# Two fused layers on one NeuronCore: head sums by ScalarE's accumulator, block products on copied partial sums, four batches' tails together, batch 0 in units, and a new order of all steps

## The chip, the cores and the metric

The kernel runs on one core of a Trainium2 chip. The core has five engines with a queue of instructions each: TensorE (PE) multiplies and transposes into the eight PSUM banks; VectorE (DVE) and ScalarE (ACT) do element work and read and write PSUM and SBUF; GpSimd (POOL) works on SBUF; SyncE (SP) issues most DMA transfers. ScalarE's and GpSimd's queues issue some transfers too. Every queue is worked off in order; semaphores hold an instruction until what it needs is done.

The metric is the device time of one execution in microseconds (us), lower is better. The kernel before takes 295.43 us, the median of 3 runs (295.1 to 296.01).

## The reference

Batch 8, 8 heads of 64, sequence 576, width C = 512; activations are float32, `w_val`, `conv_w` and `w_out` arrive as float64.

```python
kv = einsum('bhsd,bhse->bhde', k, v)
out = einsum('bhsd,bhde->bhse', q, kv)
rms = sqrt(mean(out * out, axis=-1, keepdims=True) + 1e-06)
x = (out / rms * g_norm), heads side by side          # (B, S, 512)
gate_pre[:, t] = sum over k of conv_w[k] * x[:, t - 4 + k]   # 5 taps, causal
gate = 1 / (1 + exp(-gate_pre))
val = x @ w_val
return gate * val @ w_out
```

## The kernel before

All work is written as small steps, Python functions such as `fast_product(i, p, n)`. A text, `PLAN` (lines 19 to 226), lists 1242 of them, with the buffers they take behind an `@`. The loop at the end walks this list and issues each step's instructions. So the list sets both the order in each engine's queue and the order of any two accesses to one buffer. `rooms` (line 275) holds the buffers by tag: eight PSUM banks (`bank`), rooms for gates, normalised rows (`x`), squares (`sq`) and so on.

A batch goes through these steps. Tokens come in chunks c = 0 to 3 of 128 and a tail, c = 4, of 64.

- `load_half` and `load_q` (or `load_q_rows` for batches 0 and 1) fetch k, v and q. `kv_product` (line 468) sums k^T v per head, 36 small products per half of the heads; `kv_copy` takes the result out. For batch 0 `kv_half` lays it out block by block in `kv_bd`.
- q is turned by TensorE (`turn_q_rows`, then `sort_q` copies) for batches 0 and 1 and by VectorE (`turn_q`) later on.
- `raw_pair` and `raw_tail` (batch 0: `raw_half`) multiply q by kv into two banks. `square` (line 583) squares the heads on ScalarE into a `sq` room whose 65th column per head holds the epsilon, `sums` (line 604) adds up each head on VectorE, `powers` (line 613) raises to -1/2 on GpSimd, and `normalise` (line 620) multiplies: on ScalarE one instruction per head, with the head's root as its scale; for batch 0 on VectorE.
- The normalised rows are turned into `xT` (channels on partitions): by `turn_x` and `keep_x` for batches 0 and 1 and all tails, by `turn_blocks` on VectorE and `move_blocks` otherwise. `move_blocks` issues four transfers, on GpSimd's and SyncE's queues in turn.
- `gate_start`, four `gate_tap` and `gate_end` make a gate per 128 channels.
- val: for batches 0 and 1 `val_product` (line 695), plain products. For batches 2 to 7 a scheme with seven block products in place of eight: `x_sums` and `val_sums` make sums of blocks, `val_fast` n = 0 to 6 (line 734) multiplies into three banks a, b, c, and `val_keep` (line 751) takes partial results out between products. Product 0 fills a; its copy goes to SBUF; products 2, 4 and 6 add onto a and each state is read again; c is used by products 1 and 5, b by product 3. Reads 3, 4 and 5 are VectorE adds onto the SBUF copy, the others are ScalarE copies.
- `gated` multiplies gate and val.
- Output, for pairs i of batches: `token_sums` and `weight_sums` make block sums, `fast_product` n = 0 to 6 (line 819) multiplies in the same scheme, for four groups p of 256 tokens per pair. Half bank a has a bank of its own; b and c are two halves of another (`both`, line 834). `fast_keep` (line 842) reads: ScalarE copies for n = 0, 1, 2, 6; VectorE adds for 4 (256 wide) and 5 (512 wide, b and c at once). The two 64-token tails of a pair go through `out_product` (line 772, eight products of 512 columns) and `keep_out`. `store` writes rows out in four transfers, mostly on SyncE's queue.

The float64 weights come as pairs of 32-bit words (`stage_weight`) and are made float32 by `narrow_weight` in eight steps: 0, 4, 5, 6, 7 on VectorE, 1, 2, 3 on ScalarE. `start_warm` issues products of the identity as a filler for TensorE.

Of the kernel before, what the change touches and what calls it, by code (L numbers as in the profile page):

```python
# [9 lines left out]
FP32 = mybir.dt.float32  # L10
# [5 lines left out]
P = 128  # L16
# [3 lines left out]
load_q_rows 0 1; load_q_rows 0 0; load_half v 0 0 @ 0; load_half k 0 0 @ 0; load_half v 0 1 @ 0;  # L20
load_half k 0 1 @ 0; start_warm 5 256 @ 0; warm_up; stage_weight wval 0; stage_weight wval 1;
stage_weight cw 0 @ 0; turn_q_rows 0 4 @ 1; turn_q_rows 0 3 @ 2; sort_q 0 4 @ 0; turn_q_rows 0 0 @ 3;
turn_q_rows 0 2 @ 4; sort_q 0 3; turn_q_rows 0 1 @ 5; start_warm 3 256 @ 6; load_q_rows 1 0; load_q_rows 1 1;
sort_q 0 0; stage_weight wval 2; kv_product 0 0 @ 7 0; narrow_weight cw 0 0 @ 0; load_half k 1 1; sort_q 0 2;
load_half v 1 1; kv_half 0 0; sort_q 0 1; raw_half 0 3 0 @ 1; narrow_weight cw 0 1; narrow_weight cw 0 2;
kv_product 0 1; stage_weight wval 3; narrow_weight cw 0 3; load_half k 1 0; narrow_weight cw 0 4;
narrow_weight cw 0 5 @ 0; raw_half 0 0 0 @ 2; stage_weight wout 1 @ 1; narrow_weight cw 0 6 @ 1; kv_half 0 1;
narrow_weight cw 0 7; narrow_weight wval 0 0 @ 1; raw_half 0 3 1; narrow_weight wval 0 5 @ 2;
narrow_weight wval 0 1; raw_half 0 0 1; narrow_weight wval 0 6 @ 3; turn_cw @ 6; square 0 3 @ 0;
raw_half 0 2 0 @ 3; keep_cw; square 0 0 @ 1; sums 0 3 @ 0 0; raw_half 0 2 1; narrow_weight wval 0 2;  # L30
raw_half 0 4 1 @ 4; sums 0 0; powers 0 3; load_half v 1 0; square 0 2 @ 2; raw_half 0 4 0;
narrow_weight wval 1 0 @ 0; raw_half 0 1 0 @ 5; square 0 4 @ 0; sums 0 2; narrow_weight wval 0 3;
raw_half 0 1 1; sums 0 4; load_half v 2 1 @ 0; start_warm 1 256 @ 0; narrow_weight wval 1 1;
narrow_weight wval 0 4; powers 0 2; square 0 1 @ 1; narrow_weight wval 1 5 @ 0; narrow_weight wval 1 2;
narrow_weight wval 0 7; stage_weight wout 0 @ 2; turn_q_rows 1 3 @ 7; normalise 0 3 @ 0;
narrow_weight wval 1 3; turn_q_rows 1 2 @ 6; sums 0 1; sort_q 1 3 @ 1; turn_q_rows 1 1 @ 0;
load_half v 2 0 @ 0; narrow_weight wval 2 0 @ 1; turn_x 0 3 @ 1; narrow_weight wval 1 6 @ 1; powers 0 1;
normalise 0 4 @ 1; narrow_weight wval 2 1; turn_q_rows 1 0 @ 7; load_q 2 2; normalise 0 2 @ 2; turn_x 0 4 @ 4;
keep_x 0 3; narrow_weight wval 1 4; turn_x 0 2 @ 3; keep_x 0 4; narrow_weight wval 2 2;
narrow_weight wval 2 5 @ 2; kv_product 1 1 @ 1 4; narrow_weight wval 1 7; keep_x 0 2;  # L40
narrow_weight wval 2 6 @ 3; sort_q 1 1; val_product 0 1 1 @ 3; narrow_weight wval 3 0 @ 0;
narrow_weight wval 3 5 @ 0; halo 0; normalise 0 1 @ 0; narrow_weight wval 3 1; normalise 0 0 @ 1;
narrow_weight wval 2 3; narrow_weight wval 3 6 @ 1; turn_x 0 1 @ 0; narrow_weight wval 3 2; turn_x 0 0 @ 5;
narrow_weight wval 2 4; load_half k 2 1 @ 0; val_product 0 0 1 @ 2; keep_x 0 1; narrow_weight wout 1 5 @ 2;
keep_x 0 0; narrow_weight wval 2 7; narrow_weight wval 3 3; narrow_weight wout 1 0 @ 1;
narrow_weight wout 1 6 @ 0; gate_start 0 0 @ 0; kv_product 1 0; narrow_weight wval 3 4; gate_start 0 3 @ 1;
gate_tap 0 0 3; sort_q 1 2; turn_q_rows 1 4 @ 0; narrow_weight wval 3 7; val_product 0 0 0 @ 5; load_q 2 0;
gate_tap 0 0 2; keep_val 0 0 1; gate_tap 0 3 3; gate_start 0 1 @ 2; sort_q 1 4; val_sums 2;
val_product 0 3 0 @ 6; gate_tap 0 1 3; kv_copy 1 1; kv_copy 1 0; load_q 2 1; sort_q 1 0; gate_tap 0 0 1;
raw_tail 1 @ 0 2; gate_tap 0 3 2; raw_pair 1 3 @ 1 4; square 1 4 @ 2; narrow_weight wout 0 5 @ 3;  # L50
keep_val 0 0 0; gate_tap 0 0 0; val_product 0 2 1 @ 7; gate_start 0 2 @ 3; gate_tap 0 3 1; square 1 3 @ 0;
square 1 2 @ 1; sums 1 4 @ 1 1; gate_tap 0 2 3; narrow_weight wout 1 1; powers 1 4; load_half k 2 0 @ 0;
val_product 0 1 0 @ 5; sums 1 3; keep_val 0 1 1; stage_weight wout 3 @ 0; gate_end 0 0; gate_tap 0 1 2;
powers 1 3; narrow_weight wout 1 2; sums 1 2; narrow_weight wout 1 3; val_product 0 2 0 @ 3; gated 0 0;
keep_val 0 3 0; keep_val 0 2 1; gate_tap 0 2 2; normalise 1 4 @ 2; powers 1 2; narrow_weight wout 1 4;
normalise 1 3 @ 0; raw_pair 1 1 @ 7 6; turn_q 2 0 @ 0; stage_weight wout 2 @ 1; turn_q 2 2; turn_x 1 4 @ 0;
load_q 2 3; val_product 0 3 1 @ 2; gate_tap 0 3 0; keep_x 1 4; normalise 1 2 @ 1; gate_tap 0 2 1;
narrow_weight wout 0 6 @ 2; turn_x 1 3 @ 0; keep_val 0 3 1; gate_tap 0 1 1; load_q 3 1; turn_x 1 2 @ 1;
# [172 lines left out]
def kernel(  # L231
# [104 lines left out]
    def head(hp, r):  # L336

        return r * (H // 2) + hp
# [579 lines left out]
```

## Time and profile before

| what | value |
|---|---|
| median of 3 runs | 295.43 us (295.1 to 296.01) |
| the profiled execution: span from first to last instruction | 294.9 us |
| mean granted TensorE clock | 0.993 |
| `fast_product` rows (L838), 448 | about 381 ns as a row, overlapping |
| `val_fast` rows (L747), 336 | about 407 ns as a row |
| `out_product` rows (L785), 64 | 598 ns as a row |
| `normalise` on ScalarE (L636), 252 | 56.1 us busy |
| `square` on ScalarE (L600), 70 | 21.6 us busy |
| `sums` on VectorE (L607), 40 | 24.7 us busy |
| `powers` on GpSimd (L617), 38 | 73.1 us busy |
| `gate_tap` on VectorE (L686), 128 | 100.4 us busy |
| ScalarE busy from 27 to 60, 60 to 105, 105 to 165, 165 to 225 us | 31.69, 36.99, 42.25, 41.05 us |
| VectorE busy in the same stretches | 32.49, 44.60, 59.65, 58.72 us |
| DMA read and written | 39.21 and 9.44 MB |

A profile is one execution recorded on the chip. A row such as "L838 PE MATMUL bank<-wsum,w 128x256 x4" stands for four instructions of line 838 that write a bank from the tiles wsum and w. A float32 product gives two rows. Rows of one engine can overlap: an instruction starts before the one ahead has left the pipeline, so the distance from start to start is what an engine needs for it, and a row is longer. "<-" behind a wait names what ended it. Slices are fortieths of the span, in tenths of busy time.

### The profile page before, as it was taken

How to read it: one execution, taken by the hardware profiler on the slowest of the kernel's cores; microseconds unless marked ns; L12 is line 12 of the kernel's file. 1: busy time of each engine (PE TensorE's matmuls, PEld its weight loads, DVE VectorE, ACT ScalarE, POOL GpSimd, SP SyncE). 2: the span in 40 equal slices, each digit the busy share in tenths (PEclk: the TensorE clock that was granted, in tenths of full speed). 3: DMA queues.
4: the chain of work that ended last, by engine and by line, in shares of the span. 5: the costliest groups of instructions: out<-in, count | busy, mean ns of one | idle time of the engine just before them, and what ended most of it. 6: DMA issues, size and time to landing. Idle time of an engine off the chain costs nothing.

```text
span 294.9 us, 8675 instructions
## 1 busy us (share of the span) xinstructions
PE 287.0 (97%) x3279; PEld 226.9 (77%) x3279; DVE 268.7 (91%) x483; ACT 198.7 (67%) x621; POOL 120.7 (41%) x131
## 2 busy tenths in 40 slices
PE   7999999999999999999999999999999999999994
PEld 3776878788887768878887767888887588788583
DVE  1699999999999999999999999999998999999812
ACT  2899999999786667867477576659588433723330
POOL 3067054854491477421881649021592072000020
PEclk9997999999999999999999999999999999999999
DMA  7999998886686766946789789534553170221344
GB/s 268 379 392 410 284 276 230 239 258 176 197 189 198 234 150 182 341 144 174 182 237 279 167 218 308 165 112 109 141 128 80 44 170 2 57 53 36 98 105 120
DMA packets 32009, 55.51 MB, mean 188 GB/s; under 512 B 6166, under 2 KB 14358, under 8 KB 31968
## 3 DMA queue, kind: packets, MB, share of 16 engines
q1 hardware_dynamic: 29328, 49.50, 57.2%
q0 software_dynamic: 1760, 3.43, 5.2%
q10 hardware_dynamic: 880, 2.03, 1.8%
q8 instruction: 26, 0.43, 0.6%
q14 instruction: 15, 0.12, 0.1%
HBM read 39.21 MB, written 9.44 MB: 165 GB/s over the span
## 4 chain that ended last, share of the span: by engine, by line
PE 94%; DMA 2%; ACT 1%; DVE 1%; issue 0%
PE bank L838 33%; PE bank L747 28%; PE bank L698 11%; PE bank L476 7%; PE bank L551 6%; PE bank L785 5%; PE bank L648 2%; DMA qs<-in_q_dram 2%; PE bank L563 2%; PE bank L515 1%; PE bank L464 0%; ACT wexp L409 0%; DVE x L626 0%; ACT sq L596 0%; DVE ss L607 0%; ACT wexp L407 0%
## 5 line engine op out<-in xcount | busy, mean ns | idle before, releaser
L617 POOL TENSOR_TENSOR rt<-ss,mhalf 128x8 f32<-128x8 f32 (+3 forms) x38 | 73.1, 1937 | 82.0 <-DVE ss L607 81.8
L686 DVE SCALAR_TENSOR_TENSOR gate<-xT,cwT,gate 128x576 f32<-128x576 f32 x128 | 100.4, 807 | 0.2
L636 ACT ACTIVATE x<-bank,rt 128x64 f32<-128x64 f32 x252 | 56.1, 375 | 3.5 <-POOL rt L617 3.2
L838 PE MATMUL bank<-wsum,w 128*128 128x256 f32 x192 | 47.3, 381 | 0.0
L669 POOL DMA_DIRECT2D xT<-y x48 | 26.6, 559 | 41.6 <-DVE gv L754 13.5
L838 PEld LDWEIGHTS bank<-wsum,w 128*128 128x128 f32 x192 | 36.0, 190 | 6.1 <-issue 0.8
L747 PE MATMUL bank<-xs,vsum 128*128 128x288 f32 x144 | 37.1, 407 | 0.0
L747 PEld LDWEIGHTS bank<-xs,vsum 128*128 128x128 f32 x144 | 27.3, 190 | 7.3
L698 PE MATMUL bank<-xT,wval 128*128 128x288 f32 x128 | 32.8, 411 | 0.0
L838 PE MATMUL bank<-wout,gv 128*128 128x256 f32 x128 | 32.3, 382 | 0.0
L698 PEld LDWEIGHTS bank<-xT,wval 128*128 128x128 f32 x128 | 24.0, 192 | 6.3
L693 ACT ACTIVATE gate<-gate 128x576 f32<-128x576 f32 x32 | 23.0, 727 | 7.9 <-DVE gate L686 7.8
L838 PEld LDWEIGHTS bank<-wout,gv 128*128 128x128 f32 x128 | 24.0, 190 | 3.5
L680 ACT ACTIVATE gate<-xT,cwT 128x576 f32<-128x576 f32 x32 | 25.2, 804 | 0.9 <-DVE gv L711 0.9
L747 PE MATMUL bank<-xT,wval 128*128 128x288 f32 x96 | 25.7, 406 | 0.0
L600 ACT ACTIVATE sq<-bank 128x256 f32<-128x256 f32 (+1 forms) x70 | 21.6, 400 | 6.0 <-PE bank L551 5.8
L711 DVE TENSOR_TENSOR gv<-gv,gate 128x576 f32<-128x576 f32 x32 | 23.5, 745 | 2.0 <-ACT gate L693 1.5
L607 DVE TENSOR_REDUCE ss<-sq 128x8 f32<-128x520 f32 (+1 forms) x40 | 24.7, 624 | 0.5 <-ACT sq L600 0.4
L848 DVE TENSOR_TENSOR ot<-bank,ot 128x256 f32<-128x256 f32 (+1 forms) x32 | 17.2, 546 | 8.4 <-PE bank L838 4.1
L747 PEld LDWEIGHTS bank<-xT,wval 128*128 128x128 f32 x96 | 18.2, 190 | 4.5
L854 ACT COPY ot<-bank 128x256 f32<-128x256 f32 x16 | 6.0, 376 | 22.6 <-PE bank L838 22.6
L551 PEld LDWEIGHTS bank<-kv,qT 64*64 64x64 f32 x1008 | 16.3, 135 | 4.8 <-issue 2.1
(91 smaller groups left out, 469.4 us busy)
## 6 DMA issues: line engine op xcount, KB each, us to landing
qs<-in_q_dram SPq DMA_DIRECT2D x96, 140.0 KB, 4.0
out_dram<-ot SPq DMA_DIRECT2D x136, 64.0 KB, 1.7
k<-in_k_dram SPq DMA_DIRECT2D x14, 576.0 KB, 4.9
v<-in_v_dram SPq DMA_DIRECT2D x12, 576.0 KB, 5.3
xT<-y POOLq DMA_DIRECT2D x48, 64.0 KB, 2.7
xT<-y SPq DMA_DIRECT2D x48, 64.0 KB, 2.7
y<-in_moe_w_val_dram SPq DMA_DIRECT2D x4, 512.0 KB, 11.9
w<-in_moe_w_out_dram SPq DMA_DIRECT2D x4, 512.0 KB, 7.1
```

Of the source, the lines that this page charges most:

```text
L551: nc.tensor.matmul(st["raw", b, c][r][cols, to * D:(to + 1) * D], st["qT", b][rows, hp, first:first + D], kvs[b % 2][rows, hp, :], start=T ...
L607: nc.vector.reduce_sum(out=st["ss", b][:, FIRST[c]:FIRST[c] + n], in_=st["sq", b, c][:, 0:n], axis=AX.X)
L617: nc.gpsimd.tensor_tensor(out=st["rt", b][:, which], in0=st["ss", b][:, which], in1=mhalf[:, which], op=ALU.pow)
L636: nc.scalar.activation(out=x[:, to * D:(to + 1) * D], in_=raw[:, h * D:(h + 1) * D], func=AF.Copy, scale=root[:, to:to + 1])
L669: (nc.sync if i % 2 else nc.gpsimd).dma_start(out=xTs[b % 2][i * TB:(i + 1) * TB, :, first:first + P], in_=y[a * TB:(a + 1) * TB, i])
L680: nc.scalar.activation(out=gate[:], in_=xTs[b % 2][:, jt, HALO:SX], func=AF.Copy, scale=cwT[:, K - 1, jt:jt + 1])
L686: nc.vector.scalar_tensor_tensor(out=gate[:], in0=xTs[b % 2][:, jt, tap * TB:tap * TB + S], scalar=cwT[:, tap, jt:jt + 1], in1=gate[:], op ...
L693: nc.scalar.activation(out=gate[:], in_=gate[:], func=AF.Sigmoid)
L698: nc.tensor.matmul(val[:], wval[:, kc, jt * P:(jt + 1) * P], xTs[b % 2][:, kc, HALO + n * SV:HALO + (n + 1) * SV], start=(kc == 0), stop=( ...
L711: nc.vector.tensor_tensor(out=both, in0=both, in1=st["gate", b, jt][:], op=ALU.mult)
L747: nc.tensor.matmul(st[bank, "val", b, mj][:], weights_[:, k], tokens()[:, k], start=(n in (0, 1, 3) and k == 0), stop=(k == NK // 2 - 1), ...
L838: nc.tensor.matmul(st[bank, i, p], tokens()[:, k], weights_[:, k], start=(n < 2 and k == 0), stop=(k == NK // 2 - 1), skip_group_check=True)
```

## The change

The list of steps is new (1288 steps), and these parts of the code:

- **Head sums.** For batches 1 to 7 `square` is one ScalarE instruction per head, which squares into a throw-away tile and gives the sum over the head by its accumulator. `sums` stays for batch 0 alone. `powers` gets a GpSimd add of the epsilon.
- **Copied partial sums.** In all groups (`SEEDED_VAL`, `SEEDED_OUT`), the copy of product 0 goes into bank b, and product 3 adds onto it there; read 3 is then a plain copy (for val in place of an add), and read 5 of the output an add of 256 columns. In the output a and c become the halves of one bank, and b has another bank.
- **Tails.** `keep_tail` copies each batch's 64 tail tokens into a tile; four batches give two chunks of 128, which go through the seven products as groups 4 0 and 5 0. `out_product` of tails and `keep_out` leave the list.
- **Batch 0 in units** of two chunks and half the heads: `raw_unit`, `square_unit`, `sums_unit`, `powers_unit`, `normalise_unit`, `turn_unit`, `keep_unit`; batch 0's `val_product` is split into halves that need one half of the heads each. For that, val's blocks are formed of channel blocks 0, 2 and 1, 3 (`EARLY`, `LATE`) in place of 0, 1 and 2, 3.
- **Weights.** `narrow_weight` loses step 3; step 2 is done on VectorE.
- **Engines by step.** Copies, `normalise`, `gate_start` and step 1 of `narrow_weight` take an argument that puts them on VectorE. `move_blocks` becomes two steps, one per queue.
- **Loads at the start.** `stage_weight wval 0` and `load_half v 0 0` now come ahead of q.

```diff
+    ACT_SUMS = (1, 2, 3, 4, 5, 6, 7)
+    SEEDED_OUT = {(0, 1), (1, 2), (4, 0), (2, 1), (3, 1), (0, 2), (2, 2), (1, 0), (3, 2), (1, 3), (0, 0), (1, 1), (0, 3), (2, 0), (3, 0), (2, 3), (3, 3), (5, 0)}
+    SEEDED_VAL = {(4, 0), (7, 1), (2, 1), (3, 1), (6, 1), (7, 0), (2, 0), (5, 1), (3, 0), (5, 0), (6, 0), (4, 1)}
...
+    EARLY, LATE = slice(0, NK, 2), slice(1, NK, 2)
...
+    def copy(e, out, in_):
+
+        if e:
+            nc.vector.tensor_copy(out=out, in_=in_)
+        else:
+            nc.scalar.copy(out=out, in_=in_)
...
         elif n == 2:
-            nc.scalar.activation(out=e, in_=e, func=AF.Relu, bias=biases[0:rows, 1:2], scale=-1.0)
-        elif n == 3:
-            nc.scalar.activation(
-                out=e, in_=e, func=AF.Identity, bias=biases[0:rows, 2:3], scale=-float(1 << 23))
+            nc.vector.tensor_scalar(
+                out=e, in0=e, scalar1=MOST, scalar2=float(1 << 23), op0=ALU.min, op1=ALU.mult)
...
     def square(b, c):
...
                     nc.scalar.activation(
-                        out=sq[:, to, 0:D], in_=raw[:, h * D:(h + 1) * D], func=AF.Square,
-                        accum_out=st["ss", b][:, FIRST[c] + to:FIRST[c] + to + 1])
+                        out=junk[:], in_=raw[:, h * D:(h + 1) * D], func=AF.Square,
+                        accum_out=st["ss", b][:, first + to:first + to + 1])
...
+    def root(b, which):
+        ss, rt = st["ss", b][:, which], st["rt", b][:, which]
+        if b in ACT_SUMS:
+            nc.gpsimd.tensor_scalar_add(ss, ss, D * EPS)
+        nc.gpsimd.tensor_tensor(out=rt, in0=ss, in1=mhalf[:, which], op=ALU.pow)
...
+    def raw_unit(g, i):
+
+        raw = st["unit", g, i] = ps([P, 2, C // 2], f"unit{g}_{i}")
+        for j, c in enumerate(UNIT[g]):
+            for m in range(2):
+                nc.tensor.matmul(
+                    raw[:, j, m * P:(m + 1) * P], st["qT", 0][:, 2 * i + m, c * P:(c + 1) * P],
+                    kv_bd[:, 2 * i + m, :], start=True, stop=True)
...
-    def move_blocks(b, a):
+    def move_blocks(b, a, e):
...
-        for i in range(HB):
-            (nc.sync if i % 2 else nc.gpsimd).dma_start(
+        for i in range(1 - e, HB, 2):
+            (nc.gpsimd if e else nc.sync).dma_start(
...
     def val_keep(b, mj, n, on=0):
+        seeded = (b, mj) in SEEDED_VAL
+        if seeded and n == 0:
+            st["b", "val", b, mj] = ps([P, SV], f"seed{b}_{mj}")
...
         if n == 0:
-            nc.scalar.copy(out=to(0, 0), in_=a)
+            copy(on, out=b_ if seeded else to(0, 0), in_=a)
...
+        elif n == 3 and seeded:
+            copy(on, out=to(0, 0), in_=b_)
...
+    def keep_tail(b, on=0):
+
+        if ("tail", b // 2) not in st:
+            st["tail", b // 2] = new("sq", [P, NK, P], FP32, f"tail{b // 2}")
+        first = b % GVS * S + SF
+        copy(
+            on, out=st["tail", b // 2][:, :, b % 2 * T:(b % 2 + 1) * T], in_=gv[:, :, first:first + T])
...
     def fast_product(i, p, n):
...
+        if (i, p) in SEEDED_OUT:
+            if n == 0:
+                both = ps([P, 2, C // 2], f"ac{i}_{p}")
+                st["a", i, p], st["c", i, p] = both[:, 0], both[:, 1]
+            for k in range(NK // 2):
+                nc.tensor.matmul(
+                    st[bank, i, p], tokens()[:, k], weights_[:, k],
+                    start=(n == 0 and k == 0), stop=(k == NK // 2 - 1), skip_group_check=True)
+            return
...
     def fast_keep(i, p, n, on=0):
+        seeded = (i, p) in SEEDED_OUT
+        if seeded and n == 0:
+            st["b", i, p] = ps([P, C // 2], f"b{i}_{p}")[:]
...
         if n == 0:
-            nc.scalar.copy(out=first[:, LOW], in_=a)
+            copy(on, out=b if seeded else first[:, LOW], in_=a)
+        elif n == 3:
+            copy(on, out=first[:, LOW], in_=b)
...
+        elif n == 5 and seeded:
+            add(first[:, HIGH], c)
```

The new list begins, and goes on where the groups of output products meet, like this:

```
stage_weight wval 0; narrow_weight wval 0 0 @ 0; narrow_weight wval 0 5 @ 0; load_half v 0 0 @ 0;
start_warm 1 244 @ 0; narrow_weight wval 0 1 1; narrow_weight wval 0 2; start_warm 1 246 @ 1; start_warm 1 248 @ 2;
...
narrow_weight cw 0 0 @ 1; start_warm 3 256 @ 5; start_warm 5 256 @ 6; load_q_rows 0 0; load_q_rows 0 1;
turn_q_rows 0 3 @ 7; load_half k 0 0 @ 0; narrow_weight cw 0 5 @ 2; stage_weight wval 2; load_half v 0 1 @ 0; warm_up;
...
gate_tap 1 2 3; fast_keep 0 0 1 @ 3; fast_product 0 0 2; fast_keep 0 0 2; gate_tap 1 0 3; move_blocks 2 0 0;
fast_product 0 1 2; move_blocks 2 1 0; turn_q 4 0 @ 0; fast_keep 0 1 2 @ 1; square 3 2; fast_product 0 1 3;
...
fast_keep 3 0 1 @ 2; fast_product 3 1 1; fast_keep 3 1 1 @ 0; fast_product 3 1 2; fast_keep 3 1 2 @ 3;
fast_keep 3 0 2 1 @ 1; token_sums 5 0 3 @ 2; fast_product 3 1 5; token_sums 5 0 2; fast_keep 3 1 5;
```

More of the change, by code (lines that the diff above doesn't have):

```diff
@@ L25 @@
[L25 to L41, printed above, removed]
@@ L52 @@
[L52 to L56, printed above, removed]
@@ L102 @@
-gate_start 2 0 @ 2; token_sums 0 1 0 @ 0; move_blocks 3 2; gate_start 2 2 @ 1; turn_q 4 3; normalise 3 4 @ 2;
-move_blocks 3 1; turn_q 4 1; gate_tap 2 3 3; raw_pair 4 3 @ 2 7; token_sums 0 1 1; move_blocks 3 0;
-gate_tap 2 2 3; raw_pair 4 1 @ 6 5; square 4 3 @ 2; gate_tap 2 2 2; keep_out 0 8 @ 0; fast_product 0 3 0 @ 0;
-square 4 1 @ 1; store 0 8; move_blocks 3 3; sums 4 3 @ 0 0; fast_product 0 3 1 @ 3; sums 4 1;
-fast_keep 0 3 0 @ 1; square 4 0 @ 0; gate_tap 2 3 2; powers 4 1; fast_product 0 3 3; token_sums 0 1 2 @ 2;
```

629 lines of the change are left out of this document (340 added, 289 removed).

## The prediction

> **What bounds the kernel now.** I read the page first: busy times, the slices, then the chain that ended last.
>
> ```profile
> PE 287.0 (97%) x3279; PEld 226.9 (77%) x3279; DVE 268.7 (91%) x483; ACT 198.7 (67%) x621; POOL 120.7 (41%) x131
> ...
> PE   7999999999999999999999999999999999999994
> ...
> DVE  1699999999999999999999999999998999999812
> ACT  2899999999786667867477576659588433723330
> ...
> PE 94%; DMA 2%; ACT 1%; DVE 1%; issue 0%
> ```
>
> TensorE is the bound: 94% of the chain, and every slice but the first and last is full. VectorE is as full from slice 3 to 29, yet all waits of TensorE add up to 3.5 us in the view of waits. So only three things can move the end: TensorE's own work, the time until it runs without gaps, and new waits put into its queue.
>
> Next the chain in order of time, for start and prices.
>
> ```profile
> 0.75 5.27 DMA qs<-in_q_dram
> ...
> 10.20 1.28 PE bank L476 x72
> 11.47 0.19 ACT kvbd L486
> 11.66 0.01 issue
> 11.67 0.22 ACT kvbd L486
> 11.89 0.04 issue
> 11.93 0.94 PE bank L563 x4
> ...
> 27.04 2.47 PE bank L698 x8
> ```
>
> ```profile
> 113.16 2.59 PE bank L838 x12
> ...
> 168.66 3.58 PE bank L785 x16
> ```
>
> Rows L838 are four to a `fast_product`: 2.59/12 x 4 = 0.86 us. One `out_product` is 3.58. TensorE is continuous from 27.0, the first `val_product`. Before it stand 34 transposes (0.11 each), three `kv_product` (1.21), 40 rows of L563 (0.108), ten of L648 (0.11) and 0.17 for `turn_cw`: 12.9 us of work at 27.0, a lag of 14.1. At the other end the last product stops at 290.5, and 4.3 us of copy, issue and store follow.
>
> The third view is the timeline of the last microseconds, for the banks.
>
> ```profile
> 285.82 1.24 PE L838 MATMUL bank<-wsum,w 128*128 128x256 f32 x5
> ...
> 286.90 1.03 PE L838 MATMUL bank<-wout,gv 128*128 128x256 f32 x4
> ...
> 288.01 0.37 ACT L852 COPY ot<-bank 128x256 f32<-128x256 f32 x1 [1.40 <-PE bank L838]
> ```
>
> These are product 1 of group 3 3 (the last four of five rows, done at 287.06), product 3, and the copy of what product 1 made. ScalarE idles 1.40 us and copies only at 288.01, 0.08 after product 3 ends at 287.93. Product 3 writes the other half of that bank, no byte that the copy reads. Product 4 (another bank) is not waited for. Groups 3 1, 3 2 and 2 3 show the same (copy 0.03 to 0.04 after product 3). So an access to one half of a bank is held until what the order lists before it on the other half is done.
>
> **The change, part by part.**
>
> *Tails.* Four `out_product` go: 4 x 3.58 = 14.3. Two groups of seven `fast_product` come: 14 x 0.86 = 12.1. TensorE -2.2. Beside it eight copies `keep_tail` (0.38 each on ScalarE, by L854), eight sums (0.41) and four adds (0.41) on VectorE, hidden below. Store transfers stay 16; four move from POOL's queue to SP's.
>
> *Head sums.* VectorE loses 28 reduces of 0.68 and seven of 0.41: 21.8 us. ScalarE loses 70 squares (21.6 us) and gets 252 of 64 elements, with a sum read out each. The trace has no accumulator. Nearest rows:
>
> ```profile
> 85.20 1.75 ACT L636 ACTIVATE x<-bank,rt 128x64 f32<-128x64 f32 x8 [0.75 <-POOL rt L617]
> ...
> 91.25 1.21 ACT L600 ACTIVATE sq<-bank 128x256 f32<-128x256 f32 x4 [0.47 <-PE bank L551]
> ...
> 103.56 0.48 ACT L600 ACTIVATE sq<-bank 128x128 f32<-128x128 f32 x2
> ```
>
> Start to start, a 64-wide instruction with a column operand takes (1.75 - 0.35)/7 = 0.20, a square 0.27 at 256 and 0.18 at 128, so some 0.13 at 64. Low end 0.13 (reading out is free), high end 0.40 (it costs a second such instruction). I take 0.20, the row of the same shape: 50 us (33 to 101). [...]
>
> ScalarE also loses two of three steps of `narrow_weight` (12.8), three more (2.2), `keep_out` (2.4) and 28 normalises (6.2), and gets 20 + 9 copies (11.3), `keep_tail` (3.0) and four sorts (1.5). 198.7 - 45.2 + 66.2 = 220 us, 75% of the span (203 to 270): nothing on TensorE while it stays below it. Uncovered, it is a rival. `powers` gains 35 adds on POOL (0.2 to 0.3 by the fill and select of the identity), 9 us on an engine 41% busy. From raw product to root a chunk then takes 8 x 0.20 + 0.15 + 0.25 = 2.0 us where two squares and a reduce took 1.35; its two banks are held 0.65 longer. Other products cover that, which stand between each `raw_pair` and the next user of its banks; without them it would be 28 x 0.65 = 18 us.
>
> *VectorE.* Beside the sums it loses 12 adds of 0.44 and half of 16 of 0.68 (9.5 together) and gets about 16 (one `narrow_weight` step, tail sums, copies and normalises moved to it): 253 us. Nothing, since TensorE does not wait for it now.
>
> *Copied partial sums.* Product 3 now adds onto a copy of product 0's result, so it waits for a copy. In the order at least one other product (0.86) lies between product and copy's reader in each such pair; a copy with handing over is below that, so 0. But halves a and c now share one bank, and six of seven products and five reads of a group go through it. I went through the order of steps and counted where a product follows directly on one of its own group with a read of that bank listed between (`fast_product 3 1 1; fast_keep 3 1 1; fast_product 3 1 2; fast_keep 3 1 2; ... fast_product 3 1 5`; `fast_product 2 0 5; fast_keep 2 0 5; fast_product 2 0 4`): 15 places, seven of them in the last 26 us of products. The order of before has none. By the bank rows TensorE has to stand until the read is done, all later products behind it. Price: the gap 11.47 to 11.93 is 0.46 for two copies of 0.41, 0.05 for handing over; a 0.37 copy gives 0.42, the low end. The product's drain (1.03 as a row, 0.86 in sequence) adds up to 0.17, and 0.07 goes from product to ACT: high end 0.66. I take 0.55, as weights can load in the drain: 15 x 0.55 = **+8.3** (6.3 to 9.9). [...]
>
> *Batch 0 in units, new order.* On SP `wval` 0 (0.52 MB) now goes ahead of q, on ACT's queue v 0 0 (0.59), so q (1.18) is complete at 2.3 MB in place of 1.2. The slices moved 268 and 379 GB/s, 1.98 MB by 7.4 us: q lands at about 8.2, not 6.0. Thirteen filler products cover that. k 0 0 and part of v 0 1 follow: 10.6. Then a `kv_product` 1.2, copies 0.9, `raw_unit` 0.9, on ScalarE a sort, a narrowing and the square 1.8, the sum 0.7: the first root starts near 16. POOL then has four roots of 2.0 and one of 1.2: last root 25.2, normalise, turn and keep 2.1 more, so TensorE is continuous from 27.3. By then it has done 36 transposes, two `kv_product`, 40 rows of L563, 18 of L648, `turn_cw` and three half `val_product` (0.97): 15.8, a lag of 11.5. That is -2.6; with the roots ahead of it by the 1 us that the two queues' sharing may save, -3.6. I take **-3.0** (-5 if the roots start at 14; +2.2 if q's delay passes through). `move_blocks` issues the same 96 transfers, POOL's half and SP's half apart; waiting there would hold roots, but POOL has 160 us free.
>
> **Sum**: 294.9 (span of the profiled execution) - 2.2 - 3.0 + 8.3 = 298.0. The median of the runs is 295.4, 0.5 above that execution: **298.5 us**, own range 294 to 302.
>
> **Rivals.**
> 1. *The waits cost nothing* (faster): they fall where TensorE stands anyhow, or halves are not held. 298.5 - 8.3 = 290.2 (287 to 294). For it: VectorE gets 15 us of room, and copies list right behind their products. Against it: four groups show the hold, and a continuous TensorE has no gaps to hide 15 waits. Chance 0.30.
> 2. *ScalarE becomes the bound.* From 27 to 225 the table by stretches gives it 152 us of 198; most head squares fall there: less 21.6, 9 (narrowing) and 6, plus 50 and 12, makes 177. At 0.28 per head it is full; at 0.33 it needs 210, 12 more than there is, of which the bank waits share about a third: 306. Against it: that needs a read-out as long as the square. Chance 0.13.
> 3. *The start is later, not earlier*: q's 2.2 us go through to the end: 298.5 + 3.0 + 2.2 = 303.7. For it: VectorE narrows weights between units' sums in one queue. Against: the roots' chain has the later end. Chance 0.10.
> The forecast keeps 0.47.
>
> **How the numbers follow.** A difference of 0.3% (0.9 us) is about what a measurement of this kernel tells from none. Faster: rival 1's 0.28 and 0.05 from the forecast's low end, 0.33. Same: 0.02 and 0.08, 0.10. Slower: 0.57. The range 288.5 to 305 leaves out the best part of rival 1 (0.09) and most of rival 2 (0.10).
>
> **What would show it.** Bank waits: in the waits, TensorE (or its weight loads) on ScalarE's and VectorE's reads at L838's successor, some 15 of 0.5 us, half of them in the last 30 us; if they sum to under 3 us, this step is wrong. Start: first `val_product` near 23, no gap after 27. Head sums: the square's rows 0.20 apart; ScalarE busy near 220, VectorE near 253. Tails: no 512-wide output product left. The prediction fails if TensorE's waits are as few as before, or if ScalarE is full from 30 to 200.

## The result, and the profile after

The changed kernel takes 351.08 us (median of 4 runs, 350.65 to 353.48) where the kernel before takes 295.72 (295.1 to 296.44): a ratio of 1.189, 95% interval 1.185 to 1.193. The forecast was 298.5. The profiled execution has a span of 349.2 us. Some executions of a kernel came out over 1.5% slower than its fastest; the medians of the runs below leave these out, the ranges hold all.

The page of the changed kernel, its busy times, slices and chain:

```profile
PE 300.9 (86%) x3283; PEld 235.9 (68%) x3283; DVE 257.7 (74%) x475; ACT 247.3 (71%) x1043; POOL 121.6 (35%) x164
...
PE   8799799889589948978789887987999999999794
...
DVE  3799499679659937887798797977789998653221
ACT  1889799999689995979988999698945553231210
...
PEclk9999899999899996999999999998999999999999
...
ACT 35%; PE 34%; DVE 16%; DMA 6%; issue 5%; POOL 1%; SPq 0%; DVEq 0%; ACTq 0%
```

TensorE's slices are no longer all 9: they have holes up to slice 26. The chain, 94% TensorE before, is now a third ScalarE. Most of ScalarE's slices up to 26 are at 8 or 9, and that is where TensorE's holes are. The granted clock, flat before but for one slice, has more dips. VectorE's work is what the prediction said (257.7 us for 253), ScalarE's is not (247.3 for 220).

The view of waits of the changed kernel (engine and line, what it waited for, us in total, times, longest):

```profile
PE bank L913 <- ACT bank L345: 10.0, 4, 6.1
PE bank L913 <- ACT ot L345: 10.0, 8, 3.9
...
DVE qT L509 <- DMA qs<-in_q_dram: 9.5, 4, 4.7
...
PE bank L913 <- DVE ot L937: 4.8, 5, 1.2
...
PE bank L485 <- issue: 2.8, 3, 1.2
```

Before, TensorE's waits summed to 3.5 us. Now its block products (L913) wait 20 us for ScalarE's copies (L345) and 4.8 for VectorE's adds (L937). Two rows have no counterpart before: VectorE waits for loads of q, and TensorE stands with nothing waited for ("issue").

The table by stretches, changed kernel (stretch, its length, then busy us and instructions of PE, PEld, DVE, ACT and POOL, the granted clock, DMA share and GB/s):

```profile
27.00:60.00 33.00, 28.68 (x535) 22.73 (x536) 27.71 (x56) 30.01 (x133) 15.22 (x19) 0.95 0.79 247
60.00:105.00 45.00, 36.03 (x531) 27.82 (x522) 31.44 (x56) 39.87 (x207) 24.19 (x31) 0.96 0.86 230
105.00:165.00 60.00, 50.60 (x735) 39.36 (x735) 46.22 (x79) 51.91 (x237) 27.33 (x41) 0.94 0.69 192
165.00:225.00 60.00, 52.28 (x671) 41.41 (x673) 50.33 (x87) 53.40 (x234) 29.89 (x41) 1.00 0.53 149
```

TensorE loses 30 of these 198 us, where before it lost none.

To see where the time goes, I worked out a lag for several kernels: the time less TensorE's useful work done by then. Each recorded row counts with its line's median distance from start to start, and the rows that come in quick pairs with the mean within a step: 17 ns for the 64x64 products, 224 for `out_product`. Warm-up products are left out.

| us from the start | before | changed | five outputs (e1) | places parted (e3) | before, own outputs (e4b) |
|---|---|---|---|---|---|
| 27 | 13.8 | 13.9 | 13.9 | 13.9 | 12.4 |
| 45 | 14.8 | 19.2 | 19.4 | 19.4 | 14.8 |
| 60 | 14.8 | 21.0 | 21.1 | 21.8 | 16.9 |
| 105 | 15.2 | 34.0 | 29.7 | 30.1 | 25.6 |
| 165 | 15.3 | 48.0 | 38.2 | 36.9 | 28.8 |
| 225 | 15.8 | 57.6 | 42.7 | 41.8 | 31.5 |
| 285 | 16.1 | 65.3 | 45.1 | 42.9 | 34.4 |

The kernel before hardly lags further once it is under way. The changed kernel is level with it at 27 us, behind by 4 at 45, and loses most between 60 and 225.

### The profile page after: what moved, and what is told of

It is laid out like the page before. It is cut to its first block, busy times and chain, and to the rows that moved or that the text cites. A ratio compares the mean times of both kernels' runs of the same rounds, so it can differ in the third digit from the quotient of the medians.

```text
span 349.2 us, 9163 instructions
## 1 busy us (share of the span) xinstructions
PE 300.9 (86%) x3283; PEld 235.9 (68%) x3283; DVE 257.7 (74%) x475; ACT 247.3 (71%) x1043; POOL 121.6 (35%) x164
## 4 chain that ended last, share of the span: by engine, by line
ACT 35%; PE 34%; DVE 16%; DMA 6%; issue 5%; POOL 1%; SPq 0%; DVEq 0%; ACTq 0%
PE bank L913 22%; ACT junk L606 17%; PE bank L809 8%; DVE gate L747 7%; ACT x L657 6%; DMA qs<-in_q_dram 3%; DMA k<-in_k_dram 3%; ACT qT L345 2%; ACT gate L742 2%; ACT gv L345 2%; DVE gv L772 2%; PE bank L562 2%; ACT ot L345 2%; DVE ot L937 1%; PE bank L671 1%
## 5 line engine op out<-in xcount | busy, mean ns | idle before, releaser
L913 PE MATMUL bank<-wsum,w 128*128 128x256 f32 x216 | 58.2, 400 | 21.1 <-ACT bank L345 10.0
L629 POOL TENSOR_TENSOR rt<-ss,mhalf 128x8 f32<-128x8 f32 (+1 forms) x40 | 68.7, 1722 | 19.0 <-DVE ss L682 16.1
L606 ACT ACTIVATE junk<-bank 128x64 f32<-128x64 f32 x252 | 57.5, 228 | 9.8 <-PE bank L562 2.5
L913 PEld LDWEIGHTS bank<-wsum,w 128*128 128x128 f32 x216 | 41.8, 200 | 32.4 <-ACT bank L345 12.4
L345 ACT COPY ot<-bank 128x256 f32<-128x256 f32 x65 | 25.3, 400 | 39.5 <-PE bank L913 35.5
L606 ACT ACTIVATION_READ_ACCUMULATOR junk<-bank 128x1 f32 x252 | 50.5, 200 | 0.0
L628 POOL TENSOR_SCALAR ss<-ss 128x8 f32<-128x8 f32 (+1 forms) x35 | 12.1, 346 | 83.0 <-ACT junk L606 82.0
L345 ACT COPY gv<-bank 128x288 f32<-128x288 f32 x61 | 26.1, 440 | 17.9 <-PE bank L809 17.9
L937 DVE TENSOR_TENSOR ot<-bank,ot 128x256 f32<-128x256 f32 x36 | 15.0, 419 | 28.6 <-PE bank L913 17.0
L913 PE MATMUL bank<-wout,gv 128*128 128x256 f32 x128 | 35.2, 403 | 0.4 <-DVE gv L772 0.4
L913 PEld LDWEIGHTS bank<-wout,gv 128*128 128x128 f32 x128 | 25.4, 201 | 5.8 <-DVE gv L772 1.2
L760 PEld LDWEIGHTS bank<-xT,wval 128*128 128x128 f32 x128 | 24.1, 195 | 6.6 <-ACT kv L345 0.2
L719 DVE STREAM_TRANSPOSE y<-x 128x512 f32<-128x512 f32 x24 | 16.8, 705 | 9.8 <-ACT x L657 9.8
```

Source lines behind the costliest of these rows:

```text
L345: nc.scalar.copy(out=out, in_=in_)
L606: nc.scalar.activation(out=junk[:], in_=raw[:, h * D:(h + 1) * D], func=AF.Square, accum_out=st["ss", b][:, first + to:first + to + 1])
L629: nc.gpsimd.tensor_tensor(out=rt, in0=ss, in1=mhalf[:, which], op=ALU.pow)
L760: nc.tensor.matmul(st["val", b, jt, n][:], wval[:, kc, jt * P:(jt + 1) * P], xTs[b % 2][:, kc, HALO + n * SV:HALO + (n + 1) * SV], start=( ...
L913: nc.tensor.matmul(st[bank, i, p], tokens()[:, k], weights_[:, k], start=(n == 0 and k == 0), stop=(k == NK // 2 - 1), skip_group_check=True)
L937: add = lambda out, one: nc.vector.tensor_tensor(out=out, in0=one, in1=out, op=ALU.add)
```

## The experiments

T1: ScalarE's head sums are dearer than taken and hold up what stands behind them. T2: the waits at the bank that a and c share. T3: the new order, its start and its queues. T4, formed later: TensorE runs out of instructions. T5, later: loads of q late in SyncE's queue hold up VectorE and with it TensorE. Times are medians; the kernel before took 295.4 to 295.5 beside each.

### Head sums: one output or several

What the trace showed first is the distance of two heads. ScalarE's timeline in the changed kernel (start, us, operation):

```profile
40.26 0.23 ACT L606 ACTIVATE junk<-bank 128x64 f32<-128x64 f32 x1
40.38 0.19 ACT L606 ACTIVATION_READ_ACCUMULATOR junk<-bank 128x1 f32 x1
40.61 0.22 ACT L606 ACTIVATE junk<-bank 128x64 f32<-128x64 f32 x1
```

A head is two instructions: the square, and 0.12 us later a read-out of 0.19. The next square starts 0.35 after the last, only when the read-out has ended. All heads write one tile, `junk`, and in the program each next square waits on the semaphore that the one before it raises; in the trace it starts 0.04 behind the end of the read-out (40.57 to 40.61). Four kernels test whether this wait is the price.

e1, five outputs in turn:

```diff
-    junk = const.tile([P, D], FP32, name="junk")
+    junk = const.tile([P, 5, D], FP32, name="junk")
...
-                        out=junk[:], in_=raw[:, h * D:(h + 1) * D], func=AF.Square,
+                        out=junk[:, to % 5], in_=raw[:, h * D:(h + 1) * D], func=AF.Square,
```

> The changed kernel, but the 252 head squares write five 64-wide outputs in turn instead of one. T1 (a head costs 0.35 us because each square waits for the read-out of the one before, whose output it overwrites, and ScalarE so loaded holds up the copies): the step from head to head falls from 0.347 to about 0.21 us (0.12 to the read-out, 0.093 behind it), ScalarE's heads from 87 to about 54 us, the time from 351 to about 320 us (308 to 330). T1b (the read-out itself lasts that long whoever follows): the step stays at 0.33 to 0.35 and the time at 348 to 354. T2 (the waits on the shared bank alone made the loss) and T3 (the new order and start made it): the step falls but the time stays above 343.

Measured: 329.9 us (329.3 to 331.3), 21.2 below the changed kernel. ScalarE's timeline of e1 at that time:

```profile
40.12 0.22 ACT L606 ACTIVATE junk<-bank 128x64 f32<-128x64 f32 x1
40.23 0.21 ACT L606 ACTIVATION_READ_ACCUMULATOR junk<-bank 128x1 f32 x1
40.32 0.23 ACT L606 ACTIVATE junk<-bank 128x64 f32<-128x64 f32 x1
```

The next square now starts 0.09 behind the start of the read-out: a step of 0.20 us in place of 0.35. ScalarE is busy for 225.5 us, near the 220 forecast. So T1 holds for the step, T1b falls. But 329.9 is 10 us above the 320 that T1 expected, at the upper end of its range.

e4a and e4b put the head sums alone into the kernel before: `ACT_SUMS = (1, 2, 3, 4, 5, 6, 7)`, no `sums` for these batches, order as before. e4a writes all heads of a chunk to one place, e4b each to its own columns:

```diff
-                        out=sq[:, to, 0:D], in_=raw[:, h * D:(h + 1) * D], func=AF.Square,
+                        out=sq[:, 0, 0:D], in_=raw[:, h * D:(h + 1) * D], func=AF.Square,
```

> The kernel before with one part of the change: head sums of batches 1 to 7 by ScalarE's accumulator, all heads of a chunk written to one 64-wide output, VectorE's reductions of these batches gone, order and all else as before. T1: the step from head to head is 0.35 us, ScalarE is full between 60 and 225 us, the time rises from 295.7 to about 330 us (315 to 345). T2 and T3: the time stays within 291 to 303.

> As the run with one output a chunk, but every head of a chunk writes columns of its own. T1: the step is about 0.21 us, heads take 54 us in place of the 16 of wide squares, and the time is 295 to 312 us, well under that of the run with one output. T1b: the step stays at 0.33 to 0.35 and both runs agree within 2 us. T2 and T3: 291 to 303.

Measured: e4a 353.8 us (+58.4, ratio 1.199, interval 1.195 to 1.203), e4b 315.6 (+20.2, 1.070, 1.067 to 1.072). The head sums alone, written as in the changed kernel, cost the old order more than the whole change costs, and 38 us of it is the shared output. T1 is shown. e4a's own timeline shows both steps beside each other:

```profile
41.69 0.22 ACT L385 ACTIVATE sq<-bank 128x64 f32<-128x64 f32 x1
41.81 0.19 ACT L385 ACTIVATION_READ_ACCUMULATOR sq<-bank 128x1 f32 x1
41.90 0.22 ACT L385 ACTIVATE sq<-bank 128x64 f32<-128x64 f32 x1
```

Within a chunk the squares are 0.35 apart. The one at 41.90 begins a new chunk, which writes another tile, and it starts 0.21 behind the square before it.

e4b also shows something T1 had too small: at 0.20 a head, the price I had taken, the sums still cost 20 us. e4b by stretches:

```profile
27.00:60.00 33.00, 29.81 (x466) 23.14 (x465) 27.02 (x48) 32.75 (x147) 12.32 (x15) 1.00 0.86 256
60.00:105.00 45.00, 38.46 (x546) 30.12 (x546) 33.65 (x57) 42.03 (x234) 23.24 (x28) 1.00 0.63 175
```

ScalarE, with 230 of 314 us busy in the whole, is full here (32.75 of 33, 42.03 of 45), and TensorE loses 10 us. e4c and e4d ask whether that is the reason: heads on ScalarE only in batches 3 to 7, or only in 1 and 2.

> As the run of the kernel before with own outputs for the heads (315.6 us, 20.2 above the kernel before), but head sums on ScalarE in batches 3 to 7 alone (180 of the 252 heads); batches 1 and 2 keep wide squares and VectorE's sums. T1 (it costs where ScalarE is full: 32.8 of 33 us from 27 to 60 and 42.0 of 45 from 60 to 105, where batches 1 and 2 lie): 300 to 305. Rival (each head costs the same wherever it lies): 295.4 + 20.2 x 180 / 252 = 309.8.

> The counterpart: head sums on ScalarE in batches 1 and 2 alone (72 heads). T1: 305 to 311. Rival (each head costs the same): 295.4 + 20.2 x 72 / 252 = 301.2.

Measured: 307.0 us for 180 late heads (+11.6, 0.064 a head) and 305.3 for 72 early ones (+9.9, 0.138 a head). An early head costs twice a late one, so the full stretch matters: e4d's TensorE is busy without a break from 105 to 285 us, so all its loss lies before. But late heads are not free either, and e4c lies between the two expectations. Its ScalarE is busy for 77 to 86% of the stretches from 60 to 225 us, and yet TensorE stops there 1.1 us for a norm of ScalarE and 1.3, 1.4 and 1.9 us for its copies. These four stops are about half of the 11.6 us; where the rest arises is not shown.

e2 takes ScalarE's load away from the changed kernel itself; it forms one sum per bank and leaves out the sums per head:

```diff
-                for h in range(n // 2):
-                    to = r * n // 2 + h
-                    nc.scalar.activation(
-                        out=junk[:], in_=raw[:, h * D:(h + 1) * D], func=AF.Square,
...
+                to = r * n // 2
+                nc.scalar.activation(
+                    out=junk[:, 0:n // 2 * D], in_=raw[:, 0:n // 2 * D], func=AF.Square,
```

> The changed kernel, but one square with one accumulator for each bank of heads (70 of them, 256 or 128 wide) instead of one for each head; the other sums of a bank are left at 1, so the norms are left out in part, and every other instruction stays. T1: ScalarE gives up about 87 - 70 x 0.45 = 55 us, the time falls to 300 to 315 us. T2 or T3: the time stays above 340, since the order and the 15 places at the shared bank are untouched.

Measured: 325.6 us (325.6 to 332.0; the median rests on one execution), 4 below e1, though ScalarE is busy for 204 us in place of 225. Both expectations miss: T1 alone would have given 300 to 315. Once a head takes 0.20, ScalarE's load is worth a few us at most in the new order. Something else holds it some 30 us above the kernel before.

### Bank places parted

e3 is e1 with another product put between at 15 of the 18 places where a product follows one of its own group with a read of the bank that a and c share in between, as here (the prediction counted 15; in three more the product ahead is one that fills b):

```diff
-fast_product 0 0 1; fast_keep 0 0 1 @ 3; fast_product 0 0 2; fast_keep 0 0 2; fast_product 0 1 2;
+fast_product 0 0 1; fast_keep 0 0 1 @ 3; fast_product 0 1 2; fast_product 0 0 2; fast_keep 0 0 2;
...
-fast_product 3 1 1; fast_keep 3 1 1 @ 0; fast_product 3 1 2;
+fast_product 3 1 1; fast_keep 3 1 1 @ 0; fast_product 3 1 3; fast_product 3 1 2;
```

The reason, in TensorE's timeline of the changed kernel near the end, where nothing else is in the way:

```profile
310.64 2.10 PE L913 MATMUL bank<-wsum,w 128*128 128x256 f32 x9
313.20 1.13 PE L913 MATMUL bank<-wsum,w 128*128 128x256 f32 x4 [0.46 <-ACT ot L345]
314.80 0.48 PE L913 MATMUL bank<-wout,w 128*128 128x256 f32 x1 [0.46 <-ACT ot L345]
```

Each stop is 0.46 between modelled ends and starts; from start to start it costs 0.63. Six such stops behind 312 us cost 0.63 to 0.68, a seventh 1.07.

> Five outputs in turn as in the first run, and the order changed at 15 of the 18 places where a product follows one of its own group with a read of their bank listed between: another product is put between, three places are left. T2: the gaps of TensorE before such products summed to about 18 us in the run with five outputs (0.63 to 0.68 in the last part, 0.7 to 4.2 earlier), so the time falls from 329.9 to about 313 us (308 to 318). T3 (the readers are late in VectorE's and ScalarE's queues, wherever the products stand): the gaps move to the next product of the group and the time stays at 324 to 331.

Measured: 321.3 us (319.6 to 322.6), 8.6 below e1. In the last part one such stop is left (0.67 at 314 us); of the earlier ones a stop of 4.3 us at 92 us stayed. So parting the places gains about what the forecast had for them (8.3), and half of what T2 expected here: the gaps at these places in e1 sum to some 18 us, and the largest is the one that stayed.

e6 puts copied partial sums alone into the kernel before, in the 8 groups where the order allows it (`SEEDED_OUT` and the changed kernel's `fast_product` and `fast_keep`, a `fast_keep i p 3` ahead of each `fast_keep i p 5`). It leaves part of the sum out, as I take it from the order of steps half of the copied sum in groups 0 3 and 2 1; this was not measured by itself, and the instructions are the same.

> The kernel before with copied partial sums alone, in 8 of the 16 groups of block products (those whose order allows it): a and c in one bank, product 0 copied by ScalarE into the bank of product 3, b copied out once more, VectorE's last add half as wide. The order of products is unchanged, so hardly a product follows its own group's read. T2 and the prediction (a copy costs nothing while another product covers it): 294 to 297.5 us. If the copied sums themselves cost time (product 3 waiting for its copy, ScalarE's 8 more copies): 8 x 0.3 to 0.8 us more, 298 to 302.

Measured: 303.5 us (+8.0, ratio 1.027, 1.024 to 1.029), above both. The end of its TensorE timeline:

```profile
287.05 1.13 PE L844 MATMUL bank<-wout,w 128*128 128x256 f32 x4 [0.46 <-ACT ot L335]
288.75 0.48 PE L844 MATMUL bank<-wsum,gv 128*128 128x256 f32 x1 [0.57 <-DVE ot L868]
```

Nine stops of 0.46 to 0.93 from start to start stand ahead of block products, 6.0 us together; the kernel before has none above 0.31 there. The order of products is the old one, made for a and c in different banks; once they share one, it has six places of the kind parted in e3, in groups 2 2, 3 2 and 3 3, and five of the nine stops stand there. The stop at 111.7 us (0.66) is product 3 waiting for its copy, which started only when product 1, on the other half of the bank, was done. So copied sums in this form cost time in either order, at about the price per place that was taken.

### What is left in the new order

e3 is still 26 us above the kernel before. Its waits of TensorE:

```profile
PE bank L494 <- issue: 6.1, 4, 2.2
PE bank L922 <- DVE ot L946: 6.0, 3, 4.3
PE bank L922 <- ACT ot L354: 3.2, 4, 1.5
PE bank L571 <- issue: 1.6, 1, 1.6
```

e16 joins e2's sums with e3's order, to see whether ScalarE's load matters now that the bank waits are out of the way.

> Both edits together: the order with bank places parted and one accumulator per bank of heads (70 sums in place of 252; the other sums of a bank left at 1, so the norms are left out in part). T3 (what is left, 26 us above the kernel before, lies in the order of the queues and not in ScalarE's load): 317 to 323. T1 (ScalarE's load still delays it once the bank waits are out of the way): 303 to 313.

Measured: 318.0 us (315.8 to 326.1; the median rests on two executions, 315.8 and 320.3), 3 below e3 and far above T1's 303 to 313. So ScalarE's load is worth 3 us or so of the 26 that are left, little more than the scatter, and the rest is T3's.

The stop of 4.3 us "<- DVE ot" has a chain behind it. VectorE stood 5.6 us in a `turn_q` for q, whose load SyncE had issued late, behind `move_blocks`; the add behind it in VectorE's queue was late, and TensorE waited for the add. In e3 VectorE waits 14.0 us for q between 60 and 150 us; before, never. e9 moves that one transpose behind the adds:

```diff
-turn_q 4 1;
 fast_keep 0 0 4; x_sums 2 0 @ 0; fast_keep 0 0 5; load_q 5 1; gate_tap 1 0 2;
 powers 3 1; powers 3 2; fast_product 0 1 4; fast_keep 0 1 4;
+turn_q 4 1;
```

> As the run with bank places parted, with one turn_q 4 1 moved behind four of VectorE's adds and sums (behind fast_keep 0 1 4). In that run VectorE stood 5.6 us in this transpose for a load of q that SyncE issued late, the adds behind it in its queue were late, and TensorE stood 4.3 us at 92 us and then ran at a granted clock of 0.50 for 4 us. T5 (a late load reaches TensorE through VectorE's queue): that stop goes, with its low clock, and the time falls by 4 to 7 us, from 321.3 to 314 to 317. If another wait takes its place (the q load is late for raw_pair as well, or ScalarE): 319 to 322.

Measured: 322.3 us, nothing gained. VectorE's timeline of e9:

```profile
114.99 0.46 DVE L828 TENSOR_TENSOR gv<-bank,gv 128x288 f32<-128x288 f32 x1
122.71 0.71 DVE L518 STREAM_TRANSPOSE qT<-qs 128x512 f32<-128x512 f32 x1 [7.26 <-DMA qs<-in_q_dram]
```

The stop at 92 us shrank from 4.3 to 1.1, and the next late load of q, 26 us on, held VectorE for 7.3 us and TensorE for 5.6. e11 moves the loads instead: 20 `load_q` directly behind the `turn_q` that frees their room.

> As the run with bank places parted, with 20 of the load_q (batches 3 to 7) moved in SyncE's queue to directly behind the turn_q that frees their room. In that run VectorE waited 14.0 us for q between 60 and 150 us; in the kernel before it never waited for q. T5 (loads of q stand behind move_blocks and stores in SyncE's in-order queue, and their lateness reaches TensorE through VectorE's queue): VectorE's waits for q fall below 4 us and the time from 321.3 to 308 to 317. Rival (as with the one later turn_q, other waits take their place; or move_blocks and stores now wait behind q's rooms): 318 to 323.

Measured: 329.7 us (327.4 to 334.9), worse. VectorE's waits for q fell to 5.1 us, but SyncE now stood 12.4 us for `turn_q` with `move_blocks` behind it, and TensorE stood 5.2 us in one place for ScalarE's norm. SyncE's wait alone can't be the harm, since in the kernel before SyncE stands 15.1 us for `turn_q`. T5's chain is in e3's trace; what it costs in all is not shown, since in both runs that shorten it other waits came up.

e8 tests the start, with q and k 0 0 ahead of `wval` 0:

```diff
+load_q_rows 0 0; load_q_rows 0 1; load_half k 0 0 @ 0;
 stage_weight wval 0; narrow_weight wval 0 0 @ 0;
...
-load_q_rows 0 0; load_q_rows 0 1;
 turn_q_rows 0 3 @ 7;
-load_half k 0 0 @ 0;
```

> As the run with bank places parted, with both halves of q and k 0 0 put ahead of wval 0 in SyncE's and ScalarE's queues at the start. If the start is late because q and k land late (8.9 and 12.0 us): 2 to 4 us below that run. If it is late for what follows (ScalarE's and VectorE's turns, TensorE's stops at 30 to 43 us): within 1.5 us of it, or above, as VectorE's narrowing of wval starts later.

Measured: 323.9 us (323.3 to 328.8), 2.5 above e3: TensorE then waits 3.7 us for VectorE's narrowed `cw` and 2.6 for the copy of its transpose. Putting q and k first does not mend the start.

Then the "issue" rows. In e1's TensorE timeline:

```profile
35.97 0.85 PE L562 MATMUL bank<-kv,qT 64*64 64x64 f32 x41 [0.79 <-ACT kv L345]
38.47 1.16 PE L562 MATMUL bank<-kv,qT 64*64 64x64 f32 x39 [1.64 <-issue]
```

A run of 80 such products stops for 1.64 us after 41 of them, waiting for nothing that the profile shows. The transfers from 34 to 39 us show one of 16 KB on an instruction queue; by the trace it ran from 35.8 to 36.9. Four other such stops (51, 67, 139, 169 us) also begin where a transfer of that queue ends, or up to 0.8 us behind. e7 parts the small products to test T4: one `kv_product` of batches 3 to 7, and both of batch 2, one to three block products later.

> As the run with bank places parted, with one kv_product of each of batches 2 to 6 moved one to three block products later and the two loads of the next batch that use its rooms behind it, so that fewer rows of small matmuls (a raw_pair and two kv_products are 1088 instructions with their weight loads) stand one behind the other. T4 (TensorE stands 0.9 to 1.9 us in mid-step, five to six times, because its next 16 KB of instructions come later than it uses up the last): 3 to 6 us below the run with bank places parted. T3: within 1.5 us of it, or above.

Measured: 324.6 us (323.8 to 329.2). The "issue" waits fell from 7.7 to 3.6 us in the profiled execution, which took 329.2; the time did not fall: other waits came (1.1 us for VectorE's norm, 0.9 for `kv_copy`). e10 goes the other way in the kernel before: `out_product` 0 8 and 1 8 moved from between `kv_product` and `raw_pair` to behind.

> The kernel before with out_product 0 8 and 1 8 (3.6 us each), which stand between the kv_product and the raw_pair of batches 4 and 6, moved behind the raw_pair, so that small matmuls follow on each other (864 and 672 instructions). T4 (the next 16 KB of instructions come too late when small matmuls stand together): one or two stops of 1.2 to 1.9 us in mid-step with nothing waited for, next to the waits for kv_copy (0.5 to 1.0 us a place), and 297.5 to 300.5 us. Rival (the stops of the changed kernel come from its crowded queues and not from the row of small matmuls): only the waits for kv_copy, 296 to 298, and no stop with nothing waited for above 0.4 us.

Measured: 303.6 us (+8.2), more than either expected, and without an "issue" stop:

```profile
PE bank L547 <- ACT x L632: 2.4, 2, 2.2
PE bank L547 <- DVE qT L496: 2.0, 1, 2.0
```

Without the 3.6 us of `out_product`, `raw_pair` came too early for the transposed q and for the norm that frees its bank. T4 stays unproven: its stops are in the traces of the new order, but no run gained time by removing them, and in e10 the small products stand closer together, with waits of about 2 us ahead of them, and without one.

### The tails

e14 puts half of this part into the kernel before: the tails of batches 4 to 7, two `out_product` replaced by seven `fast_product` among the last products, with tails, sums and outputs in the rooms of k and v.

> The kernel before with one part of the change alone, the tails of batches 4 to 7 together: out_product 2 8 and 3 8 (2 x 3.58 us) go, seven block products of 0.86 (6.04) on copied tails come, placed among the last products; tails, their sums and outputs lie in the rooms of k and v, which are free by then. The prediction's term, half of it: -1.1 us, 293.5 to 295. Rival (out_product also covered waits, as its move in the run with small products together suggests): 295.5 to 299.

Measured: 299.2 us (ratio 1.012, 1.010 to 1.015). TensorE's work fell by 1.1 us (28 rows at 0.216 in place of 32 at 0.224), but it stood 1.4 us where `out_product` 2 8 had covered a sum of VectorE, and the last stores queued. SyncE's rows at the end of e14's timeline:

```profile
284.12 1.93 SPq L890 DMA_DIRECT2D out_dram<-v  x4
...
288.05 1.77 SPq L890 DMA_DIRECT2D out_dram<-v  x4
...
289.87 5.32 SPq L890 DMA_DIRECT2D out_dram<-ot  x8
```

The span ends 6.5 us after the last product, 4.3 before. e15 sends the tails' stores through POOL's queue and `x_sums 6 3` ahead of one `turn_blocks`.

> As the run with the tails of batches 4 to 7 together, with two edits at the places that its trace showed late: the two stores of the tails go through POOL's queue (in that run SyncE issued them, 1.9 us each, ahead of the last stores, and 6.5 us lay between the last product and the end where the kernel before has 4.3), and x_sums 6 3 goes ahead of one turn_blocks in VectorE's queue (TensorE stood 1.4 us for it). Tails' term holds (-1.1): 294 to 295.5 us. Rival (the place of out_product was worth more than its work): 296 to 298.5.

Measured: 297.7 us (1.007, 1.005 to 1.010). Better by 1.5, still above the kernel before: TensorE now waits 1.7 us for VectorE's adds of val, which it does not in the kernel before, and 4.9 us lie behind the last product. `out_product`'s place was worth more than its work. No run here is below the kernel before.

## Why the prediction was wrong

- **Head sums: this step failed.** "I take 0.20, the row of the same shape: 50 us" and "nothing on TensorE while it stays below" its span. The 0.20 is right for a head with its own output (e1), but the changed code writes every head to one tile and pays 0.347, 87 us in all. That stands in the diff and was not weighed: here an output that is overwritten is a wait of ScalarE for itself. Rival 2 came nearest ("at 0.33 ... 306") and was given 0.13, because it "needs a read-out as long as the square". It came true for another reason: the read-out takes no longer than foreseen (0.09 to the next start in e1), but the next square waits for its end. The rival's price was too small as well: 12 us of missing ScalarE time were counted, the old order lost 58 (e4a). The second half of the step failed alone too: at 0.20, with ScalarE 73% busy in all, e4b lost 20 us. About half of this comes from heads in 27 to 105 us, where ScalarE is full, since weights are narrowed there as well (e4d); the other half comes later, where it is not full but copies and norms are late behind the heads (e4c). Cover was judged over 198 us; by stretch the first half could have been seen, the second only from what each copy waits for.
- **Copied partial sums: right in the mechanism, the size in part by luck.** The reads do hold products at the shared bank. 0.55 a place was taken within 0.42 to 0.66; the undisturbed stops cost 0.63 to 0.68, about the top of that range. Parting 15 places gave 8.6 us where the term was 8.3, but that is no confirmation of 15 x 0.55: a place in the middle costs what the reader is late, 6.3 us at 125 us in the changed kernel, where the copy stands behind head sums in ScalarE's queue. In the changed kernel block products wait 24.8 us for reads in all.
- **Start: foreseen as a gain, measured as a loss.** Foreseen were -3.0 and no gap after 27 us. The first `val_product` started at 25.8 (forecast 23). The lag, foreseen at 11.5 against 14.1, was 13.9 against 13.8 at 27 us and 4.4 worse at 45: stops of 0.65 and 0.79 for ScalarE's copies, 1.64 for nothing that the profile shows, and 3.4 us at half clock behind them.
- **Tails: right in TensorE's work** (-1.1 for half, as expected), wrong in effect: the blocks removed were cover, and the stores came late at the end (+3.7, +2.3).
- **Order: left out.** The sum went from TensorE's work and listed waits only. With one output per head in turn and the bank places mended, e3 stands 31 us above the sum without the bank term (321.3 against 290.2). About 7.6 of these are the start (3.0 foreseen, 4.6 lost), and some 22 lie between 45 and 285 us. Late loads of q, adds and copies late in their queues, and stops without a named wait are in the traces there. How the 22 divide is open: e9 and e11 show that a wait taken out there is replaced by the next.

Of the 52.6 us between forecast and result, 21.2 are shown to be the shared output, and some 7.5 are the start by the table of lags. The bank places took what was forecast for them. The other 24 lie in the new order; e16 puts 3 or so of them on ScalarE's load at 0.20 a head, and what makes up the rest is not shown.

## What to carry to other kernels

Before pricing a row of small instructions, look at what each of them writes: one scratch output shared by all makes each wait for the one before, here 0.35 us in place of 0.20. An engine that is to take on work has to be checked in every stretch by itself, and for what stands behind the new work in its queue. A block of work that is removed has to be checked as cover for what stands behind it. In the order measured here a single wait taken out was worth little, because the next one stood behind it (e7, e9, e11).

## What the runs showed of the hardware that was not expected

**The clock dropped behind some stops.** The changed kernel around its stop at 89 us (stretch, length, TensorE's busy time and rows, granted clock, DMA share, GB/s):

```profile
88.00:90.00 2.00, 1.38 (x7) 1.00 1.14 301
90.00:92.00 2.00, 0.00 (x0) 1.00 0.73 184
92.00:94.00 2.00, 0.76 (x2) 0.75 0.80 233
94.00:96.00 2.00, 2.00 (x7) 0.50 0.98 264
96.00:98.00 2.00, 2.00 (x10) 0.90 1.04 267
```

Behind the stop of 3.9 us the clock lacks 0.25, 0.50 and 0.10 over three stretches of 2 us, so by my estimate it costs about 1.7 us more than itself. Less idle time was followed by a low clock too: in e1 two stops of 0.79 and 1.64 us within 3.3 us by 0.50 from 39 to 42 us, and a single stop of 2.5 us at 121 us by 0.50 to 0.53 from 124 to 127. Behind stops of 1.82 and 1.97 us at 170 and 209 us in the changed kernel it stayed at 1.00. The traces have 3.4 us at half clock in the kernel before (24.3 to 27.7), five such lengths in the changed kernel, three in e1 and two in e3, the end of each run aside.

**TensorE stopped beside instruction transfers.** Five stops of 0.7 to 1.6 us in e1 begin where a 16 KB instruction transfer of about 1 us ends or up to 0.8 us behind, and last until 1.2 to 1.6 us after it. The kernel before has as many such transfers, 26, and no such stop. That TensorE ran out of instructions in e1 is an inference from the times; no run tests it by itself.

**Reading the accumulator** overlaps what follows: in e1, at 40 us, rows of 0.19 to 0.25 us, 0.09 from its start to the next start. In the changed kernel, where the next square writes the same tile, it is 0.23.
